# The first unit of a feed-forward layer is split in two halves, with the second unit between them

## The chip, the core and the metric

The kernel is one program on one core of a Trainium2 chip. Its five engines are TensorE (matrix products; PE in the profile, PEld for its loads of weights), VectorE (DVE), ScalarE (ACT), GpSimd (POOL) and SyncE (SP, which only issues DMA transfers here). Engines run side by side, each through its own list of instructions in a fixed order, and wait for each other by semaphores. The metric is the device time of one execution in microseconds.

## The reference, cut to what matters

Three layers in a row, all float32:

```python
# 1. landmark attention: 4 batches, 8 heads, 576 tokens, 64 wide; 32 landmarks
q_lm, k_lm = q.reshape(B,H,32,18,64).mean(3), k.reshape(B,H,32,18,64).mean(3)
A, Bm, C = softmax(q @ k_lm.T / 8), softmax(q_lm @ k_lm.T / 8), softmax(q_lm @ k.T / 8)
Z = Bm.T / (norms of Bm);  6 times: Z = 2*Z - Z @ Bm @ Z
x = (A @ Z @ C @ v)                       # rearranged to 2304 tokens x 512
# 2. feed-forward with mish: 512 -> 2048 -> 512
h = x @ w_in;  x = (h * tanh(softplus(h))) @ w_out
# 3. top-2 of 8 experts, 512 -> 1024 -> 512
noisy = x @ w_gate + softplus(x @ w_noise) * noise
for e in experts: out[tokens of e] += weight * (relu(x @ w1[e]) @ w2[e])
```

## The kernel before, in words

**Products.** Every large product is done in three pieces, with each operand split into a high and a low part (names ending in h and l, and pairs such as `wo`): high x high, high x low, low x high.

**Attention and fold.** For each of the 4 batches, `attention` makes two things. One is a small matrix W (`wt`, written at L571), which takes a serial chain of softmaxes and six products (L548 to L554). The other is the softmax A: `soften` (L415 to L439) ends in the pairs `ah` and `al`. The product A·W·w_in is taken as A·(W·w_in). `fold` makes W·w_in in four blocks `gt` of 512 columns for each batch (L700 on TensorE, L707 on ScalarE, L709 on VectorE).

**Units and steps.** The 2304 tokens are 8 units of 288, and a batch has two units. The feed-forward layer of a unit is 8 steps of 256 of the 2048 hidden columns; step s belongs to unit s // 8. In a step TensorE makes the hidden columns (L733, 12 matmuls; called "up" below), ScalarE and VectorE apply mish (L746 to L771, ending in `gh` and `gl`), and TensorE multiplies by `w_out` (L788 to L790, 24 matmuls; "down"), adding over the 8 steps into four PSUM banks (`ps_acc`). The blocks of w_in and w_out arrive as float64 bits in integers and are rebuilt as float32 on VectorE: L599, L601, L603 (`widen`), and for w_out also L660 and L662. That is done once, during the first units; w_in goes back to device memory and is read again for later batches.

**Routing and experts.** After the last step of a unit, `route` copies the sums out (L839), turns them (L851, 12 transposes), picks two experts for each token (some 40 small VectorE instructions, L877 to L1008) and scatters the rows to per-expert slots in device memory (L1012, GpSimd). `zeros` fills the slots and the output with zeros before, also from GpSimd. From 486 us on, 16 expert jobs of 8 steps follow (L1151 up, L1172 to L1174 down). Each job has a first part of 384 or a second part of 256 slots; `gather` reads its rows, `entries` its list of tokens and weights (`ent`), and `give` scales the result and scatters it into the output (L1181, L1185).

**What sets the order.** Each piece is a coroutine that yields the engine and a rough cost for its next instruction. A planner (`Order.run`) keeps a clock for each engine and takes, of the instructions ready at that time, the one with the earliest due time. Due times come from `due_hidden(s)` and `due_moe(s)` and from the offsets in the table `DU`. The result is a fixed list for each engine. `keep_warm` (L589) puts small matmuls without use wherever TensorE would be free before batch 0 is ready.

Rings bound the buffers: one pair of PSUM banks for up, four banks `acc` for down, three `gh`, four `ld` (loads of q, k, v).

Of the kernel before, what the change touches and what calls it, by code (L numbers as in the profile page):

```python
# [21 lines left out]
U = 288  # L22
# [43 lines left out]
class Order:  # L66
# [105 lines left out]
    w7=0.03, t0=145.6, t1=9, t2=4.8, m0=566.3, win=67.3, wo=4.1, att=84.6, grp=73, sof=-40.6, fet=191.2, fev=157.4,  # L172
    mkU=132.3, fold=-30.7, up=-7.6, down=27.3, mish=22.6, route=-30.6, r6=24.9, r7=-94.1, send=-11.1, rows=-251.1,
    sc=-182.2, sc6=846.5, yT=-119.9, rein=-163.9, rl=-134.9, zero=204.2, w=0, lists=136.5, wts=68.3, spl=-514.8,
    gath=399.6, turn=-379.2, fin=-286.6, part=287.7, mish2=-40.6, mdown=93.9, st1=3, st2=2, st3=2,
# [3 lines left out]
def due_hidden(s):  # L179
    return DU["t0"] + DU["t1"] * min(s, 8) + DU["t2"] * max(s - 8, 0)  # L180
# [34 lines left out]
class Kern:  # L215
# [63 lines left out]
    def fill(self, dst, src, nbytes):  # L279

        yield op("G", 1.1)
        self.nc.gpsimd.dma_start(dst, src)
        yield dma(nbytes)
# [8 lines left out]
    def attention(self, b):  # L292
# [48 lines left out]
        def group(hg):  # L341
# [67 lines left out]
            o.spawn(soften(hg), due - DU["sof"])  # L409
# [33 lines left out]
        def make_AT():  # L443
            tk = yield get(self.r_AT, 2)
            for i in range(2):
                self.t_AT[2 * b + i] = tk + i
                self.AT[2 * b + i] = (
# [56 lines left out]
        o.spawn(make_AT(), due - DU["sof"])  # L504
# [104 lines left out]
    def conv_in(self):  # L609
# [24 lines left out]
        for i in range(4, 16):  # L634
# [5 lines left out]
            o.spawn(widen(i // 4, i % 4, raw, self.r_raw, tk, [1]), due_hidden(i // 2) - DU["win"])  # L640

    def reload_in(self):
        for b in range(1, B):
            for fb in range(4):
                for c in range(4):
                    yield wait(self.kept[fb, c])
                    self.o.cur.late = due_hidden(16 * b + 2 * fb) - DU["rein"]
# [4 lines left out]
    def conv_out(self):  # L652
# [13 lines left out]
        for f in range(NF):  # L666
# [10 lines left out]
            o.spawn(split(f, raw, t, ring, tk), due_hidden(f // 2) + DU["down"] - DU["wo"])  # L677


    def fold(self):  # L680

        o, V, A, T = self.o, self.V, self.A, self.T
        for b in range(B):
            yield wait(self.got_WT[b])
            for fb in range(4):
                o.cur.late = due_hidden(16 * b + 2 * fb) - DU["fold"]
# [28 lines left out]
    def hidden(self, s):  # L715

        o, V, A, T, P = self.o, self.V, self.A, self.T, self.np_
        u, f = s // (NF // 2), 2 * (s % (NF // 2))
# [8 lines left out]
        for i in range(2):  # L727
            yield op("T", 0.772)
# [9 lines left out]
        if u % 2 and f % 4 == 2:  # L738
            o.put(self.r_gt, self.t_gt[b, fb])
# [37 lines left out]
        if f == 0:  # L777
            self.t_acc = yield get(self.r_acc, 4)
            self.acc = [self.bank("acc") for _ in range(4)]
        acc = self.acc  # L780
        for i in range(2):
            yield wait(self.got_wo[f + i])
            hi, lo = self.wo[f + i]
            for c in range(4):
                if c % 2 == 0:
                    yield op("T", 0.737)
                n = slice(128 * c, 128 * c + 128)
                T.matmul(acc[c][:, :U], hi[:, n], gh[:, i], start=f + i == 0, stop=False)  # L788
                T.matmul(acc[c][:, :U], hi[:, n], gl[:, i], start=False, stop=False)  # L789
                T.matmul(acc[c][:, :U], lo[:, n], gh[:, i], start=False, stop=f + i == NF - 1)  # L790
# [14 lines left out]
    def zeros(self):  # L805


        yield wait(self.downed[2])
# [5 lines left out]
        for i, c in enumerate(range(0, CAP, U)):  # L814
            n = min(U, CAP - c)
            for e in range(NE):
                dst = slots[e, c : c + n].rearrange("(n p) x -> p n x", p=min(n, 96))
                src = zero[: min(n, 96)].unsqueeze(1).broadcast_to([min(n, 96), max(n // 96, 1), D + LW])
                yield from self.fill(dst, src, n * 4 * (D + LW))
            self.o.set(self.filled[i])  # L820
        yield wait(self.downed[20])
# [6 lines left out]
    def route(self, u, acc, ta):  # L828
# [8 lines left out]
        for c in range(4):  # L837
            yield op("A", cp(U), DU["yT"] - self.o.cur.late + due_hidden(8 * u + 7))
            A.copy(yT[:, c, :], acc[c][:, :U])  # L839
            o.put(self.r_acc, ta + c)  # L840

        def send():
# [4 lines left out]
            for i in range(3):  # L847
                for q in range(4):
                    yield op("V", cv(384), DU["rows"] if u >= NU - 2 else 0.0)
# [5 lines left out]
        o.spawn(send(), due_hidden(8 * u + 7) + DU["send"])  # L855
        yield wait(self.routed[u - 1] if u else self.emptied)
        if u < len(self.filled):
# [598 lines left out]
```

## Time and profile before

| | us |
|---|---|
| median of 3 runs | 966.08 (962.16 to 966.98) |
| the profiled execution | 968.66 |
| span of its instructions | 966.8 |
| TensorE busy | 914.0 |
| VectorE busy | 625.7 |
| ScalarE busy | 457.6 |

The span runs from the first to the last instruction; the execution is 1.9 us longer than its span, and 2.6 us longer than the median. TensorE's busy time counts the warm-up matmuls before 57 us, and matmuls are pipelined, so a busy stretch is not the same as a full one. The granted clock is given as a share of 2.4 GHz: 0.50 is 1.2 GHz.

### The profile page before, as it was taken

What the parts mean: (1) busy time and instruction counts of PE and PEld (TensorE: products, weight loads), DVE (VectorE), ACT (ScalarE), POOL (GpSimd) and SP (SyncE); (2) the same over time, 40 slices, a digit from 0 to 9 for tenths busy, and PEclk for the clock granted to TensorE, in tenths of its full rate; (3) what the DMA queues carried; (4) which work ended last, traced back from release to release, by engine and by line L of the source; (5) the groups of instructions that cost most, each with busy time, mean ns of one, the idle gap of its engine ahead of it and who ended that gap; (6) DMA issues with size and microseconds to landing.
All of it is one profiled execution on the core that took longest, in us unless ns stands there. A gap on an engine that the chain in (4) does not pass through costs nothing. (4 is left out here: it accounts for less than half of the span.)

```text
span 966.8 us, 18134 instructions
## 1 busy us (share of the span) xinstructions
PE 914.0 (95%) x7135; PEld 799.1 (83%) x7135; DVE 625.7 (65%) x1519; ACT 457.6 (47%) x825; POOL 136.4 (14%) x129
## 2 busy tenths in 40 slices
PE   9979768999999998999999989999999999999995
PEld 7767656878886877889898979899989899999984
DVE  6999689566986669486958466646565555445411
ACT  2247655667766686588853233333333223323210
POOL 0002100223101200202020412101121011111102
PEclk9989989999999999999999999999999999999998
DMA  8677950565406410323243667666556355464103
GB/s 303 198 256 255 360 209 3 152 192 173 194 7 200 164 53 2 115 67 86 58 153 91 153 191 162 148 169 143 135 118 158 109 111 125 98 165 94 17 3 51
DMA packets 70075, 131.62 MB, mean 136 GB/s; under 512 B 13696, under 2 KB 34784, under 8 KB 69984
## 3 DMA queue, kind: packets, MB, share of 16 engines
q1 hardware_dynamic: 56960, 96.16, 32.6%
q0 software_dynamic: 13024, 34.25, 15.1%
q8 instruction: 58, 0.95, 0.4%
q14 instruction: 33, 0.27, 0.1%
HBM read 91.94 MB, written 39.48 MB: 136 GB/s over the span
## 5 line engine op out<-in xcount | busy, mean ns | idle before, releaser
L1151 PE MATMUL ps_up<-xh,mw 128*128 128x256 f32 (+1 forms) x1024 | 265.5, 312 | 2.8 <-ACT mw L1039 2.1
L1151 PEld LDWEIGHTS ps_up<-xh,mw 128*128 128x128 f32 x1024 | 183.1, 189 | 15.5 <-ACT mw L1039 2.5
L1160 ACT ACTIVATE gh<-ps_up 128x384 fp32r<-128x384 f32 (+1 forms) x128 | 56.1, 438 | 285.7 <-PE ps_acc L1173 161.6
L1162 DVE SCALAR_TENSOR_TENSOR gl<-ps_up,gh 128x384 fp32r<-128x384 f32 (+1 forms) x128 | 62.7, 490 | 170.1 <-ACT gh L1160 169.9
L788 PE MATMUL ps_acc<-gh,wo 128*128 128x288 f32 x512 | 159.2, 311 | 5.3 <-ACT gh L768 5.0
L1151 PE MATMUL ps_up<-xl,mw 128*128 128x384 f32 (+1 forms) x512 | 159.3, 311 | 0.0
L789 PE MATMUL ps_acc<-gl,wo 128*128 128x288 f32 x512 | 153.2, 299 | 2.8 <-DVE gl L771 2.8
L790 PE MATMUL ps_acc<-gh,wo 128*128 128x288 f32 x512 | 152.7, 298 | 0.2 <-DVE wo L662 0.2
L733 PE MATMUL ps_h<-ah,gt 128*128 128x288 f32 x512 | 127.3, 306 | 15.7 <-ACT mh L746 15.2
L1172 PE MATMUL ps_acc<-mw,gh 128*128 128x512 f32 x320 | 126.5, 395 | 0.0
L1173 PE MATMUL ps_acc<-mw,gh 128*128 128x512 f32 x320 | 126.4, 395 | 0.0
L1174 PE MATMUL ps_acc<-mw,gl 128*128 128x512 f32 x320 | 125.8, 393 | 0.0
L1185 POOL DMA_INDIRECT out<-yp,off x40 | 67.0, 1674 | 376.9 <-DVE yp L1181 278.3
L788 PEld LDWEIGHTS ps_acc<-gh,wo 128*128 128x128 f32 x512 | 97.9, 191 | 25.5 <-issue 13.2
L733 PEld LDWEIGHTS ps_h<-ah,gt 128*128 128x128 f32 x512 | 90.0, 191 | 32.5 <-ACT mh L746 21.5
L1151 PEld LDWEIGHTS ps_up<-xl,mw 128*128 128x128 f32 x512 | 96.7, 189 | 10.0
L789 PEld LDWEIGHTS ps_acc<-gl,wo 128*128 128x128 f32 x512 | 98.0, 191 | 3.8 <-DVE gl L771 3.8
L1041 DVE TENSOR_TENSOR mw<-mraw,mw 128x1024 fp32r<-128x1024 f32 x72 | 87.8, 1223 | 18.5 <-ACT mw L1039 17.9
L790 PEld LDWEIGHTS ps_acc<-gh,wo 128*128 128x128 f32 x512 | 97.9, 191 | 0.4 <-DVE wo L662 0.4
L1012 POOL DMA_INDIRECT slots<-rr,sl x48 | 47.7, 994 | 336.4 <-DVE rr L1008 319.4
L1039 ACT CAST mw<-mraw 128x1024 fp32r<-128x1024 f32 x72 | 74.6, 1042 | 3.4 <-DMA mraw<-in_ew 3.4
L733 PE MATMUL ps_h<-al,gt 128*128 128x288 f32 x256 | 76.0, 297 | 0.0
(189 smaller groups left out, 1384.9 us busy)
## 6 DMA issues: line engine op xcount, KB each, us to landing
mraw<-in_ew SPq DMA_DIRECT2D x72, 512.0 KB, 4.1
win<-win_d SPq DMA_DIRECT2D x48, 256.0 KB, 3.4
xg<-slots SPq DMA_DIRECT2D x160, 64.0 KB, 3.1
slots<-zero POOLq DMA_DIRECT2D x16, 580.5 KB, 20.0
raw<-in_w_in SPq DMA_DIRECT2D x16, 512.0 KB, 4.7
raw<-in_w_out SPq DMA_DIRECT2D x16, 512.0 KB, 6.3
kT<-in_kT SPq DMA_DIRECT2D x8, 576.0 KB, 6.9
qT<-in_qT SPq DMA_DIRECT2D x8, 576.0 KB, 7.3
```

Source lines behind the costliest of these rows:

```text
L733: T.matmul(hp[:, i, :U], gt[:, x, hg, n : n + 128], AT[y][:, hg, :], start=k == 0, stop=k == 5)
L788: T.matmul(acc[c][:, :U], hi[:, n], gh[:, i], start=f + i == 0, stop=False)
L789: T.matmul(acc[c][:, :U], hi[:, n], gl[:, i], start=False, stop=False)
L790: T.matmul(acc[c][:, :U], lo[:, n], gh[:, i], start=False, stop=f + i == NF - 1)
L1039: self.A.copy(w[:, 0], raw)
L1041: self.V.tensor_tensor(out=w[:, 1], in0=raw, in1=w[:, 0].bitcast(F32), op=OP.subtract)
L1151: T.matmul(h[:, :n], w[:, i, 128 * c : 128 * c + 128], x[j][:, c, :n], start=k == 0, stop=k == 11)
L1162: self.V.scalar_tensor_tensor(out=gl[:, :n], in0=hp[:, :n], scalar=0.0, in1=gh[:, :n].bitcast(F32), op0=OP.max, op1=OP.subtract)
L1172: T.matmul(a, g[0][:, n], w[:, 0, 512:], start=first, stop=False)
L1173: T.matmul(a, g[0][:, n], w[:, 1, 512:], start=False, stop=False)
L1174: T.matmul(a, g[1][:, n], w[:, 0, 512:], start=False, stop=last)
L1185: st = self.G.indirect_dma_start(out=self.out[:, :], out_offset=bass.IndirectOffsetOnAxis(ap=off[:, b : b + 1], axis=0), in_=y, in_offset= ...
```

## The change

The step order is now a list `STEPS`: the first four steps of unit 0, all eight of unit 1, the last four of unit 0, and then units 2 to 7 as before. The four sums of the first half of unit 0 are copied from PSUM to a buffer of the ring `ld` (`set_aside`, four ScalarE copies), and added again when unit 0 ends (four VectorE additions in place of four ScalarE copies). Unit 1 is routed before unit 0. The zero fill covers only the second part of each expert's slots, 8 transfers of 516 KB each, and starts after step 5 in place of step 2. The due times and costs are new numbers, the softmax A of batch 0 has a due time of its own (`sof0`), and so have the expert lists (`ent`).

```diff
 DU = dict(
-    w7=0.03, t0=145.6, t1=9, t2=4.8, m0=566.3, win=67.3, wo=4.1, att=84.6, grp=73, sof=-40.6, fet=191.2, fev=157.4,
+    w7=0.4, t0=-24.6, t1=8.83, t2=2.01, m0=786.2, win=-65.7, wo=-244.7, att=486.3, grp=199.1, sof=-304.1,
...
+STEPS = [(0, f) for f in range(0, NF // 2, 2)] + [(1, f) for f in range(0, NF, 2)] + [(0, f) for f in range(NF // 2, NF, 2)]
+STEPS += [(u, f) for u in range(2, NU) for f in range(0, NF, 2)]
+UNITS = [1, 0] + list(range(2, NU))
...
-            o.spawn(soften(hg), due - DU["sof"])
+            o.spawn(soften(hg), due - DU["sof0" if head else "sof"])
...
-        if f == 0:
+        if begin:
             self.t_acc = yield get(self.r_acc, 4)
...
+        if end and f < NF - 2:
+            ts = yield get(self.r_ld)
+            o.spawn(self.set_aside(acc, self.t_acc, ts), due_hidden(s) + DU["down"] - DU["sp"])
...
+    def set_aside(self, acc, ta, ts):
+        part = self.ap.tile([128, 2, S], F32, name="part", tag="ld", bufs=4)
+        self.part, self.t_part = part.rearrange("p a (b n) -> p (a b) n", n=U), ts
+        for c in range(4):
+            yield op("A", cp(U))
+            self.A.copy(self.part[:, c], acc[c][:, :U])
+            self.o.put(self.r_acc, ta + c)
...
-        yield wait(self.downed[2])
+        yield wait(self.downed[DU["zst"]])
...
-        for i, c in enumerate(range(0, CAP, U)):
...
+        slots = slots[:, CAPA:].rearrange("e (n p) x -> e p n x", p=128)
+        for e in range(NE):
+            src = zero.unsqueeze(1).broadcast_to([128, CAPB // 128, D + LW])
+            yield from self.fill(slots[e], src, CAPB * 4 * (D + LW))
...
-            yield op("A", cp(U), DU["yT"] - self.o.cur.late + due_hidden(8 * u + 7))
-            A.copy(yT[:, c, :], acc[c][:, :U])
+            if u:
+                yield op("A", cp(U), late)
+                A.copy(yT[:, c, :], acc[c][:, :U])
+            else:
+                yield op("V", 0.37, late)
+                V.tensor_tensor(out=yT[:, c, :], in0=acc[c][:, :U], in1=self.part[:, c], op=OP.add)
...
-            self.o.spawn(self.job_entries(j), due_moe(FE * j + 4))
+            self.o.spawn(self.job_entries(j), due_moe(FE * j + 4) - DU["ent"])
```

Three places show what the new order is. In the changed program line numbers are higher by 19 to 39: L619 to L623 are `widen`, L720 and L729 the fold, L755 up, L810 to L812 down.

**TensorE, before the first step.** Before, the third fold block (`ps_g_778`) and the first up step (`ps_h_867`), with 49 pairs of warm-up rows between them, of which one stands:

```order
L700 MATMUL ps_g_778<-win_465,wt_665 32x512 x2
L700 MATMUL ps_g_778<-win_546,wt_665 32x512 x2
L589 LDWEIGHTS onesb_82
L589 MATMUL ps_h_128<-onesb_82 96x256
...
L733 MATMUL ps_h_867<-ah_136,gt_697 128x288
L733 MATMUL ps_h_867<-al_137,gt_697 128x288
```

Now, from the last warm-up on:

```order
L609 LDWEIGHTS onesb_82
L609 MATMUL ps_h_128<-onesb_82 96x256
L720 MATMUL ps_g_683<-win_145,wt_650 32x512 x2
L720 MATMUL ps_g_683<-win_187,wt_650 32x512 x2
L720 MATMUL ps_g_701<-win_310,wt_650 32x512 x2
L720 MATMUL ps_g_701<-win_375,wt_650 32x512 x2
L755 MATMUL ps_h_721<-ah_138,gt_682 128x288
```

No warm-up matmul stands between the folds any more (219 in place of 325 in all), and the first up step follows the second fold block.

**VectorE, batch 0.** Before, the softmax results `al` stand behind both parts of the first fold (`gt_697`):

```order
L709 TENSOR_TENSOR gt_697<-ps_g_728,gt_697 128x512
L603 SCALAR_TENSOR_TENSOR win_710<-raw_657,win_710 128x512
L423 TENSOR_SCALAR sA_127<-sA_127 128x18
L427 TENSOR_TENSOR A1_291<-A1_291,sA_127 128x576
L425 RECIPROCAL sA_127<-sA_127 128x18
L432 STREAM_TRANSPOSE Af_794<-A1_291 128x576
...
L439 TENSOR_TENSOR al_139<-Af_811,ah_138 128x288
```

Now they stand inside the six products of W (`X2`):

```order
L574 SCALAR_TENSOR_TENSOR X2_572<-X2_551,ps_g_557 128x192
L458 TENSOR_TENSOR al_139<-Af_540,ah_138 128x288
L623 SCALAR_TENSOR_TENSOR win_310<-raw_186,win_310 128x512
L574 SCALAR_TENSOR_TENSOR X2_592<-X2_572,ps_g_578 128x192
L458 TENSOR_TENSOR al_137<-Af_504,ah_136 128x288
...
L729 TENSOR_TENSOR gt_682<-ps_g_701,gt_682 128x512
```

The softmax moved ahead of the fold, and nine or ten blocks of weights that stood ahead of it moved behind it.

**VectorE, W of batch 1.** Before, W (`wt_2087`) stands among the routing of unit 0 (`rd`, `sa`, `sl`):

```order
L977 TENSOR_SCALAR rd_2113<-pk_2100 96x6
L980 SCALAR_TENSOR_TENSOR rd_2113<-pk_2100,rd_2113 96x6 x2
L771 SCALAR_TENSOR_TENSOR gl_2117<-mh_1897,gh_2110 128x576
L983 SCALAR_TENSOR_TENSOR sa_2127<-ek_1929,pk_2100 96x6
L571 COPY wt_2087<-ps_g_2114 128x2x32
L986 SCALAR_TENSOR_TENSOR sl_2145<-rd_2113,sa_2127 96x6
L571 COPY wt_2087<-ps_g_2115 128x2x32
```

Now it stands among the last blocks of w_out, and the first transposes of a route (`rr`) come behind it:

```order
L621 SCALAR_TENSOR_TENSOR t_1754<-raw_1753,t_1754 128x512
L591 COPY wt_1841<-ps_g_1842 128x2x32
L775 TENSOR_SCALAR me_1865<-mh_1852 128x576
L591 COPY wt_1841<-ps_g_1843 128x2x32
...
L682 TENSOR_TENSOR wo_117<-raw_1845,wo_117 128x512
...
L890 STREAM_TRANSPOSE rr_2011<-yT_1977 32x4x3x32
```

The first route moved from before W of batch 1 to behind it; part of w_out moved the other way.

## Rows read from the trace of the kernel before

**Rows 1.** Busy time by stage (stretch, length, engines, PE clock, DMA share, GB/s).

```profile
0.00:57.00 57.00, 55.76 (x631) 44.17 (x631) 46.88 (x113) 12.70 (x30) 1.39 (x11) 1.00 0.74 254
57.00:174.00 117.00, 90.34 (x872) 75.27 (x876) 100.59 (x226) 74.91 (x136) 9.78 (x14) 0.93 0.58 204
181.00:300.00 119.00, 116.42 (x1165) 99.15 (x1165) 82.27 (x220) 76.94 (x148) 24.46 (x31) 0.99 0.47 155
507.00:967.00 460.00, 446.23 (x2532) 401.04 (x2530) 238.22 (x531) 139.87 (x233) 73.60 (x46) 0.99 0.50 118
```

**Rows 2.** The same view, the stretches around batch 1.

```profile
67.00:71.00 4.00, 3.72 (x14) 3.40 (x15) 3.98 (x8) 2.46 (x5) 0.00 (x0) 0.50 0.92 314
115.00:132.00 17.00, 5.29 (x28) 4.82 (x26) 9.83 (x16) 6.99 (x11) 0.00 (x0) 0.80 1.00 381
132.00:174.00 42.00, 35.13 (x480) 28.70 (x484) 37.84 (x115) 24.28 (x49) 0.00 (x0) 0.96 0.06 21
```

**Rows 3.** TensorE in time: start, length, engine, line, what, count, wait before.

```profile
51.25 5.64 PE L589 MATMUL ps_h<-onesb 128*96 128x256 bf16 x49
57.05 0.37 PE L733 MATMUL ps_h<-ah,gt 128*128 128x288 f32 x1
67.10 0.61 PE L788 MATMUL ps_acc<-gh,wo 128*128 128x288 f32 x1 [4.65 <-ACT gh L768]
180.70 0.30 PE L790 MATMUL ps_acc<-gh,wo 128*128 128x288 f32 x1
180.84 0.29 PE L733 MATMUL ps_h<-ah,gt 128*128 128x288 f32 x1
508.23 0.94 PE L866 MATMUL ps_g<-wgn,yT 128*32 128x16 f32 x72
```

**Rows 4.** Who TensorE waited for, 120 to 200 us (sum, times, longest).

```profile
PE ps_h L733 <- ACT mh L746: 7.8, 1, 7.8
PE ps_g L356 <- DVE ql L327: 4.5, 1, 4.5
```

**Rows 5.** VectorE in time: fold, softmax result, w_out block, W of batch 1.

```profile
49.23 0.68 DVE L709 TENSOR_TENSOR gt<-ps_g,gt 128x512 fp32r<-128x512 f32 x1
56.26 0.45 DVE L439 TENSOR_TENSOR al<-Af,ah 128x288 fp32r<-128x288 f32 x1
118.77 0.43 DVE L599 TENSOR_SCALAR raw<-raw 128x512 int32<-128x512 int32 x1 [5.63 <-DMA raw<-in_w_out]
173.40 0.21 DVE L571 COPY wt<-ps_g 128x64 f32<-128x64 f32 x1
```

**Rows 6.** Who VectorE waited for, 57 to 175 us.

```profile
DVE raw L599 <- DMA raw<-in_w_out: 5.6, 1, 5.6
DVE ql L327 <- DMA qT<-in_qT: 1.6, 1, 1.6
DVE kl L327 <- DMA kT<-in_kT: 1.2, 1, 1.2
```

**Rows 7.** Groups by line, whole span: busy us, mean ns of one, idle before.

```profile
L851 DVE STREAM_TRANSPOSE rr<-yT 32x384 f32<-32x384 f32 x96 | 54.6, 568 | 12.3 <-DMA slots<-rr,sl 5.9 <-ACT yT L839 4.2
L763 DVE SCALAR_TENSOR_TENSOR mh<-me,mh 128x576 f32<-128x576 f32 x64 | 48.3, 754 | 18.5 <-ACT me L761 17.6
L603 DVE SCALAR_TENSOR_TENSOR win<-raw,win 128x512 int32<-128x512 int32 x16 | 10.9, 682 | 0.0
L901 DVE TENSOR_REDUCE m<-nz 96x3 f32<-96x24 f32 x16 | 2.7, 167 | 0.2
L839 ACT COPY yT<-ps_acc 128x288 f32<-128x288 f32 x32 | 12.2, 400 | 5.4 <-PE ps_acc L790 5.4
```

**Rows 8.** DMA issues: transfer, queue, count, KB of one, us to landing.

```profile
slots<-zero POOLq DMA_DIRECT2D x16, 580.5 KB, 20.0
ent<-slots SPq DMA_DIRECT2D x8, 6.0 KB, 4.1
```

**Rows 9.** Who TensorE waited for, 500 to 600 us.

```profile
PE ps_up L1151 <- ACT mw L1039: 2.1, 1, 2.1
```

More of the change, by code (lines that the diff above doesn't have):

```diff
@@ L171, with first, last_of @@
 DU = dict(
[L172 to L175 removed]
+    w7=0.4, t0=-24.6, t1=8.83, t2=2.01, m0=786.2, win=-65.7, wo=-244.7, att=486.3, grp=199.1, sof=-304.1,
+    fet=257.9, fev=58.6, mkU=153.2, fold=27.3, up=-50.3, down=-14.1, mish=-15.0, route=-92.7, r6=101.7, r7=682.0,
+    send=202.4, rows=-900, sc=94.3, sc6=897.1, yT=-473.0, rein=-280.7, rl=217.1, zero=279.7, w=0.02, lists=392.0,
+    wts=175.3, spl=-347.7, gath=446.0, turn=-496.0, fin=-159.3, part=152.9, mish2=291.8, mdown=337.6, st1=1,
+    st2=1, st3=1, t3=3.09, sp=379.3, sof0=131.7, zst=5, zot=17, ent=-467.4,
 )
 def due_hidden(s):
[L180 removed]
+    return DU["t0"] + DU["t1"] * min(s, 4) + DU["t3"] * min(max(s - 4, 0), 8) + DU["t2"] * max(s - 12, 0)
+STEPS = [(0, f) for f in range(0, NF // 2, 2)] + [(1, f) for f in range(0, NF, 2)] + [(0, f) for f in range(NF // 2, NF, 2)]
+STEPS += [(u, f) for u in range(2, NU) for f in range(0, NF, 2)]
+UNITS = [1, 0] + list(range(2, NU))
+END = {u: STEPS.index((u, NF - 2)) for u in UNITS}
+AT_F = {f: min(s for s, (u, g) in enumerate(STEPS) if g == f // 2 * 2) for f in range(NF)}
+def first(b, fb):
+    return min(s for s, (u, f) in enumerate(STEPS) if u // 2 == b and f // 4 == fb)
+def last_of(b, fb):
+    return max(s for s, (u, f) in enumerate(STEPS) if u // 2 == b and f // 4 == fb)
 def due_moe(s):
@@ L503, in attention @@
         o.spawn(make_U(), due - DU["mkU"])
-        o.spawn(make_AT(), due - DU["sof"])
+        o.spawn(make_AT(), due - DU["sof0" if head else "sof"])
         for hg in range(2):
@@ L646, in reload_in @@
                     yield wait(self.kept[fb, c])
-                    self.o.cur.late = due_hidden(16 * b + 2 * fb) - DU["rein"]
+                    self.o.cur.late = due_hidden(first(b, fb)) - DU["rein"]
                     yield from self.chunk_in(fb, c)
@@ L685, in fold @@
             for fb in range(4):
-                o.cur.late = due_hidden(16 * b + 2 * fb) - DU["fold"]
+                o.cur.late = due_hidden(first(b, fb)) - DU["fold"]
                 self.t_gt[b, fb] = yield get(self.r_gt)
@@ L727, in hidden @@
         for i in range(2):
[L728 removed]
+            yield op("T", 0.786)
             n = 128 * (f % 4 + i)
@@ L813, in zeros @@
         slots = self.slots[: NE * CAP].rearrange("(e c) x -> e c x", e=NE)
-        for i, c in enumerate(range(0, CAP, U)):
[L815 to L821, printed above, removed]
+        slots = slots[:, CAPA:].rearrange("e (n p) x -> e p n x", p=128)
+        for e in range(NE):
+            src = zero.unsqueeze(1).broadcast_to([128, CAPB // 128, D + LW])
+            yield from self.fill(slots[e], src, CAPB * 4 * (D + LW))
+        self.o.set(self.filled)
+        yield wait(self.downed[DU["zot"]])
         rows = self.out.rearrange("(p n) x -> p n x", p=128)
@@ L1286, in run_all @@
         self.routed_a = Event()
-        self.filled = [Event() for _ in range(0, CAP, U)]
+        self.filled = Event()
         self.AT, self.WT, self.win, self.gt = {}, {}, {}, {}
```

40 lines of the change are left out of this document (23 added, 17 removed).

## The prediction

> **What bounds the kernel now.** I read the chip's time by stage first, then what TensorE waited for, then what VectorE did there. In the expert stage (507 to 967 us) TensorE is busy 446.2 of 460 us, and between 181 and 300 us 116.4 of 119 [rows 1]: both are TensorE's, and a faster VectorE buys nothing there. Between 57 and 174 us it is not so. TensorE is busy 90.3 of 117 us, VectorE 100.6 [rows 1], and the two longest stalls lie side by side in 115 to 132 us, where TensorE works 5.3 of 17 us [rows 2]: 7.8 us for ScalarE's mish, which itself waits for VectorE, and 4.5 us for the split queries of batch 1 [rows 4]. VectorE works only 9.8 us of those 17 [rows 2]. It waited 5.6 us for a block of w_out, which ended at 118.8 us [rows 5], and 1.6 and 1.2 us for the queries and keys of batch 1 [rows 6], while the DMA engines were busy the whole time (share 1.00 [rows 2]) with the zero fills: 16 transfers of 580.5 KB, 20.0 us each from issue to landing [rows 8]. So the path up to W of batch 1 is VectorE's list, stretched by a DMA jam. W is written at 173.4 us [rows 5]; only then can W·w_in of batch 1 be folded, and step 16, the first of batch 1, starts at 180.84 us [rows 3]. From there on TensorE is the limit. What the change is worth is therefore: how much earlier W of batch 1 is ready, less the TensorE work that has been pushed behind that point.
>
> **The change part by part.**
>
> *VectorE's work ahead of W of batch 1.* Before, 46.9 us of it lie in 0 to 57 and 100.6 in 57 to 174 [rows 1], in all 147.5 of 174 us; 26.5 us are idle, 10.1 of them before 57. Counted in the two orders, the new list has these fewer instructions ahead of W: the 12 transposes of the first route (12 x 0.568 = 6.8 us [rows 7]); 29 small routing instructions (the nearest row is 0.167 us [rows 7], 4.8 at most); two mish products and one of the pairs' low parts (3 x 0.754 = 2.3 [rows 7]); and six blocks of weight rebuilding (6 x 0.68 = 4.1 [rows 7]). That is 18.0 by durations; neighbouring small instructions overlap by some hundredths of a microsecond, and I take 16. Nothing of it vanishes, it only comes later: between 181 and 300 us VectorE is busy 82.3 of 119 us [rows 1], so 36.7 are free to take 16.
>
> *The fill.* 8 x 516 KB = 4.1 MB in place of 16 x 580.5 KB (9.3 MB) and eight smaller ones: about 0.4 of the bytes. It also starts after step 5 instead of step 2, and in the new order of the queues the loads of batch 1's second keys and queries are issued ahead of it, so that they are not caught in it. VectorE's 8.4 us of DMA waits [rows 6] go to 0.4 of that, 3.4 us, a gain of 5.0. From below, all 8.4 could go; from above, the w_out block may still meet the fill and none go. The other 8.0 us of idle time after 57 us and the 10.1 before it I leave as they are.
>
> So W comes 16 + 5.0 = 21.0 us earlier, at about 153 us.
>
> *TensorE's debt.* At step 16 the old order has done 13 of the 16 down steps and one route's products; the new one 12 and none. One down step is 24 matmuls, of which two neighbours start 0.14 us apart (180.70 and 180.84 [rows 3]), 3.4 us; a route's products are 0.94 us [rows 3]. These 4.3 us of work are still owed: 21.0 - 4.3 = 16.7 us. If TensorE has idle time later to hide them, nothing is lost, but there are only 2.6 us in 181 to 300 [rows 1], so I charge all.
>
> *Setting the sums aside.* Four ScalarE copies of 0.40 us [rows 7] and four VectorE additions in place of four copies. ScalarE is busy 74.9 of 117 us [rows 1] and hides them. What TensorE feels is one more hand-over of the four banks, in which the first copy has to be done before a bank is used again: 0.4 us. If that cover is gone, all four: 1.6. An up step and a fold block stand between the two down steps in the order, so the cost could also be zero. The buffer taken from `ld` until unit 0 ends leaves three for loads of batch 1 and 2; should a load of batch 1 wait for it, it would add to the idle time of VectorE, which the range holds.
>
> *The start.* Before, warm-ups run from 51.25 to the first up step at 57.05 [rows 3], because the softmax result that the step needs ends at 56.7 [rows 5], after the second part of the fold at 49.9 [rows 5]. Now the softmax stands ahead of the fold, and the first step should begin at 48 to 50 us. I cost this at nothing of its own: the stretch is VectorE's, and the work it does first is already in the sum. A gain here would appear only as VectorE idling less.
>
> *The expert stage.* Its first step waits 2.1 us for weights [rows 9]; the last routing is spread differently, and I take half of it, 1.0, as gained; bounds 2.1 lost or gained. Then 446.2 us of TensorE work [rows 1] are the same.
>
> Sum: 16.7 - 0.4 + 1.0 = 17.3 us off the profiled execution's 968.66, which gives 951.4. That execution was 2.6 us above the median of the three runs, 966.08, so the median should be 966.08 - 17.3 = 948.8, say 949.
>
> Bounds. The best for W: of the 16.4 us idle after 57 only 5 stay (11.4 gained) and half the idle time of the head goes with the earlier start (5): 16 + 11.4 + 5 - 4.3 = 28.1, and 2.1 at the experts: 30.2, 936. The worst without a new mechanism: no idle time goes, 16 - 4.3 - 1.6 = 10.1, and 2.1 lost at the experts: 8.0, 958.
>
> **The rivals.**
>
> *More of the idle time goes (932 to 943).* For it: TensorE and ScalarE had work for VectorE 8 us earlier, and the old 8.0 us of other idle time are hand-overs in a chain with only one or two steps in flight. With no route in between, mish now follows mish. Against it: the weights still have to come in at 16 + 16 blocks, with the DMA engines 74% busy before 57 us [rows 1].
>
> *The DMA jam moves and stays (about 962 to 968, no change).* The DMA share is already high before the fill [rows 1], and a fill of 4.1 MB still keeps the engines full for some 10 us at the 381 GB/s of rows 2. If the w_out loads and the earlier loads of batch 2 meet in it, VectorE idles 8.4 us as before and another 8.4 beside, and 10.1 - 8.4 = 1.7 are left: 964. By the Trainium skill ("DMA: Bandwidth & Descriptors", section "Queues, rings and completion order"), a DMA engine takes turns packet by packet between the queues that have work. By that rule a load is slowed as long as any fill is under way, and it is the time of the fill, not its place behind, that counts; a load issued within it is no faster than before. Rows 6 and 8 agree with such sharing: the loads crept rather than stopped. I give it little, since the fill is shorter by 0.6.
>
> *TensorE falls to its lower clock at the early start (955 to 963).* The clock was granted at 0.50 in 67 to 71 us [rows 2], 1.2 GHz, right behind a gap of 4.65 us in TensorE's work [rows 3]. With the warm-ups cut off at 48 us and folds and up steps waiting for VectorE, gaps of that size may recur between 45 and 60 us, and work there takes twice as long. The Trainium skill ("TensorE: Matmul & The Clock Gate", "What's actually happening") says that the throttled state is the default and activity releases it; the drop at 67 us agrees. Against a price: TensorE has some 9 us of work in that stretch, so at half speed it loses at most 9 us, and it waits for VectorE there anyway. 949 + 9 = 958.
>
> *The lists of the experts come too late (slower).* The lists of tokens and weights now have a due time 467 later than their place in the job. VectorE's scaling of a job's result and so TensorE's four banks wait for the list. A list lands in 4.1 us [rows 8]; with the 1 us of instructions around it a late one costs a job about 5.5 us of TensorE. The gain of 17 is used up from the fourth of 16 jobs on; eight late jobs cost 44, and 966 - 17 + 44 = 993. Against it: in the two orders the list instructions stand at the same expert step, within one.
>
> **How the numbers follow.** My forecast, 943 to 955, has 58%; more idle time gone (932 to 943) 18%; the lower clock or small losses (955 to 962) 10%; no change 7%; late lists or another mechanism that makes it slower 7%. The likeliest is 949; its own range 943 to 955. Leaving out the late lists, the jam and the last few of the best case, the range is 934 to 962. A measurement can tell 0.5%, 4.8 us, from no change: faster is below 961.2, slower above 970.9. So faster 0.85, same 0.08, slower 0.07.
>
> **What would show it.** Right: the first up step starts at 48 to 50 us; VectorE writes W of batch 1 near 153 us and step 16 starts about 160 to 164; the waits of 7.8 and 4.5 us are below 3 each; the fill's transfers take well under 20 us each; in 181 to 300 TensorE stays busy above 97%; the expert stage lasts as long as before, within 2 us. Wrong: W of batch 1 is written at 165 us or later (the idle time has moved, or the softmax moved the fold back), or the earlier step 16 is given back before 507 us because VectorE, with the route behind it, is late for the mish of steps 16 to 24; or TensorE waits for `yp` or the lists in the expert stage.

## The result and the profile after

| | before | changed |
|---|---|---|
| median, us | 965.78 (962.16 to 966.98, 4 runs) | 951.27 (950.15 to 955.68, 4 runs) |
| the profiled execution | 968.66 | 950.15 |
| span | 966.8 | 948.3 |

The changed kernel takes 0.9865 of the time, with a 95% interval of 0.9824 to 0.9905: 14.5 us less between the medians, 18.5 between the two profiled executions. Measured a second time, beside the experiments, it was 0.9845 (0.982 to 0.987).

The stages of the changed kernel, with the columns of [rows 1]:

```profile
0.00:57.00 57.00, 52.77 (x560) 37.86 (x560) 46.89 (x112) 15.80 (x36) 1.38 (x11) 0.91 0.66 238
57.00:143.00 86.00, 76.53 (x720) 63.00 (x721) 82.82 (x174) 64.05 (x121) 6.07 (x8) 0.98 0.68 235
57.00:174.00 117.00, 106.67 (x1006) 86.63 (x1007) 108.72 (x234) 87.65 (x162) 6.07 (x8) 0.99 0.59 203
115.00:132.00 17.00, 16.84 (x216) 15.24 (x215) 16.44 (x45) 13.46 (x27) 4.08 (x6) 1.00 0.97 345
181.00:300.00 119.00, 113.00 (x1198) 95.71 (x1199) 90.88 (x236) 78.51 (x147) 22.45 (x24) 0.99 0.43 147
490.00:948.00 458.00, 440.61 (x2444) 396.37 (x2442) 236.94 (x535) 136.34 (x229) 74.05 (x46) 0.99 0.49 118
```

In 57 to 174 us TensorE is busy 106.7 of 117 us (90.3 before [rows 1]) and VectorE 108.7 (100.6). In 115 to 132 us, where TensorE worked 5.3 us [rows 2], it now works 16.8, though the DMA engines are just as full (0.97). The next two views show who TensorE waited for in 57 to 174 us, and who VectorE waited for in 57 to 144 us (sum, times, longest):

```profile
PE ps_h L755 <- ACT mh L768: 3.6, 2, 2.1
PE ps_g L409 <- DVE gt L729: 1.9, 1, 1.9
PE ps_acc L812 <- DVE wo L682: 1.6, 2, 1.4
PE ps_acc L810 <- ACT wo L680: 1.6, 2, 0.9
```

```profile
DVE gl L793 <- ACT gh L790: 2.0, 4, 1.2
DVE t L619 <- DMA raw<-in_w_out: 0.5, 1, 0.5
DVE gt L729 <- ACT gt L727: 0.3, 1, 0.3
DVE wo L682 <- ACT wo L680: 0.3, 1, 0.3
```

The stalls of 7.8 and 4.5 us [rows 4] are gone (the longest wait for mish that is left is 2.1 us), and of VectorE's 8.4 us of DMA waits [rows 6] 0.5 are left. Four marks in time (start, length, engine, line, what):

```profile
42.53 0.40 PE L755 MATMUL ps_h<-ah,gt 128*128 128x288 f32 x1
142.82 0.21 DVE L591 COPY wt<-ps_g 128x64 f32<-128x64 f32 x1
152.87 0.29 PE L755 MATMUL ps_h<-ah,gt 128*128 128x288 f32 x1
194.74 2.31 DVE L890 STREAM_TRANSPOSE rr<-yT 32x384 f32<-32x384 f32 x4 [4.37 <-DMA slots<-rr,sl]
```

The first up step starts at 42.5 us (57.05 [rows 3]), W of batch 1 is ready at 143.0 (173.6 [rows 5]), and step 16 starts at 152.87 (180.84 [rows 3]). A transfer of the fill now takes 9.8 us from issue to landing (median; 20.0 [rows 8]). The last mark is where part of the lead is lost again: VectorE waits 4.4 us with transposes of the second routed unit, for scatters of the first. At the start of the expert stage (470 to 560 us) TensorE waits for VectorE and ScalarE, where before it had 2.1 us [rows 9]:

```profile
PE ps_up L1190 <- DVE mw L1080: 3.2, 4, 1.4
PE ps_up L1190 <- DVE gl L1201: 2.1, 1, 2.1
PE ps_up L1190 <- ACT mw L1078: 1.7, 1, 1.7
```

To see where the time goes I count, for each kernel, TensorE's work done by a time: every matmul that has started, warm-ups left out, at the mean interval between starts on its line in the kernel before. How waits are kept out of that mean moves an entry by 1 to 2 us, and differences along a row by less. The lead over the kernel before's trace, in us:

| by | 60 | 100 | 140 | 180 | 200 | 240 | 300 | 480 | 560 | 600 us |
|---|---|---|---|---|---|---|---|---|---|---|
| changed | 4.0 | 1.5 | 15.6 | 23.4 | 18.2 | 20.8 | 18.5 | 23.3 | 17.2 | 21.7 |
| changed, plain steps (e1) | 5.7 | -3.0 | 3.0 | 9.5 | 6.4 | 10.5 | 3.1 | -0.8 | -2.8 | 2.2 |
| changed, full fill (e2) | 4.0 | 1.5 | 15.1 | 15.6 | 13.3 | 14.7 | 7.6 | 8.3 | -1.9 | 3.1 |
| before, smaller fill (e3) | 0.8 | 2.1 | 5.9 | 11.2 | 7.1 | 11.5 | 5.7 | 5.4 | 1.5 | 5.8 |
| before, late route (e5) | 1.3 | 2.4 | -0.7 | 2.3 | 1.6 | -11.1 | -15.6 | -14.6 | -13.9 | -18.9 |
| split after six steps (e6) | 4.0 | 1.7 | 5.5 | 10.2 | 6.5 | 9.2 | 1.8 | -10.1 | -10.1 | -8.2 |
| new steps, old numbers (e9) | 1.7 | 1.0 | 15.8 | 4.9 | -10.7 | -24.1 | -26.3 | -30.1 | -30.7 | -35.2 |

TensorE's last matmul ends at 935.3 us in the changed kernel and at 956.0 before, a lead of 20.7; from there to the end are 13.0 us (10.8 before), which leaves 18.5.

### The profile page after: what moved, and what is told of

Read it like the earlier page. It is cut to its first block, busy times and chain, and to the rows that moved or that the text cites. A ratio compares the mean times of both kernels' runs of the same rounds, so it can differ in the third digit from the quotient of the medians.

```text
span 948.3 us, 17922 instructions
## 1 busy us (share of the span) xinstructions
PE 903.3 (95%) x7029; PEld 785.4 (83%) x7029; DVE 627.6 (66%) x1523; ACT 457.1 (48%) x825; POOL 128.2 (14%) x113
## 5 line engine op out<-in xcount | busy, mean ns | idle before, releaser
L810 PE MATMUL ps_acc<-gh,wo 128*128 128x288 f32 x512 | 161.7, 316 | 2.5 <-ACT wo L680 1.6
L812 PE MATMUL ps_acc<-gh,wo 128*128 128x288 f32 x512 | 152.0, 297 | 1.6 <-DVE wo L682 1.6
L755 PE MATMUL ps_h<-ah,gt 128*128 128x288 f32 x512 | 126.8, 306 | 12.5 <-ACT mh L768 9.7
L810 PEld LDWEIGHTS ps_acc<-gh,wo 128*128 128x128 f32 x512 | 97.1, 190 | 30.0 <-issue 19.3
L1224 POOL DMA_INDIRECT out<-yp,off x40 | 65.1, 1628 | 350.7 <-DVE yp L1220 269.3
L755 PEld LDWEIGHTS ps_h<-ah,gt 128*128 128x128 f32 x512 | 90.7, 193 | 25.2 <-ACT mh L768 14.6
L1190 PEld LDWEIGHTS ps_up<-xl,mw 128*128 128x128 f32 x512 | 96.3, 188 | 10.5
L812 PEld LDWEIGHTS ps_acc<-gh,wo 128*128 128x128 f32 x512 | 97.1, 190 | 2.0 <-DVE wo L682 2.0
L1051 POOL DMA_INDIRECT slots<-rr,sl x48 | 50.8, 1058 | 347.4 <-DVE rr L1047 224.8
L755 PE MATMUL ps_h<-al,gt 128*128 128x288 f32 x256 | 76.6, 299 | 0.0
```

The costliest lines, as they stand in the source:

```text
L755: T.matmul(hp[:, i, :U], gt[:, x, hg, n : n + 128], AT[y][:, hg, :], start=k == 0, stop=k == 5)
L810: T.matmul(acc[c][:, :U], hi[:, n], gh[:, i], start=begin and i == 0, stop=False)
L1190: T.matmul(h[:, :n], w[:, i, 128 * c : 128 * c + 128], x[j][:, c, :n], start=k == 0, stop=k == 11)
L1224: st = self.G.indirect_dma_start(out=self.out[:, :], out_offset=bass.IndirectOffsetOnAxis(ap=off[:, b : b + 1], axis=0), in_=y, in_offset= ...
```

## The experiments

The experiments ran on different chips. The kernel before took 966.0 us beside e5, e7, e8 and the second run of the changed kernel, 974.3 beside e1 to e4, 977.4 beside e6, e9 and e10, and 977.1 beside e12. So kernels are compared by their ratio to the kernel before on the same chip. The changed kernel was not run on the three slower chips; that its 0.9845 holds there too is taken, not shown.

The eight traces from the slower chips have something that the six taken where before takes 966 us lack: pauses of TensorE, VectorE and ScalarE whose end the profile puts down to no engine and no transfer (`issue` or `remote` where the name of a releaser would stand). Counting those over 0.3 us, a trace from a slower chip has 9 to 21 of them, 13 to 46 us over the three engines, and the six others have one, of 0.3 us. The first comes at 166 us in e3 and e9, between 189 and 197 in e2, e4, e10 and e12, at 228 in e1 and at 298 in e6. The lead is taken against one trace of before from the faster chip. Up to the first pause it is the kernel's own; behind it the chip's losses are in it too.

**The changed kernel again.**

> The changed kernel unchanged, beside the other kernels of this call, so that they can be compared with it on the same chip. If the gain does not depend on the chip, it is 0.983 to 0.990 of the kernel before.

951.54 us, 0.9845 (0.982 to 0.987). W of batch 1 is ready at 142.4 us, and step 16 starts at 152.2, as in the first trace.

**e1: the changed kernel with plain steps.**

```diff
-STEPS = [(0, f) for f in range(0, NF // 2, 2)] + [(1, f) ...] + [(0, f) for f in range(NF // 2, NF, 2)]
...
-UNITS = [1, 0] + list(range(2, NU))
+STEPS = [(u, f) for u in range(NU) for f in range(0, NF, 2)]
+UNITS = list(range(NU))
```

> The changed kernel, with the steps again in the plain order (unit 0 whole, then unit 1; no sums set aside, route of unit 0 first); its due numbers and its smaller fill stay, and its VectorE list again has no route work ahead of W of batch 1. Theory A (the gain is VectorE's list: W of batch 1 comes early because the route and some weight blocks stand behind it and the DMA waits are gone): W of batch 1 still near 143 us, and the time 948 to 956, as the changed kernel's 951. Theory B (the interleaved steps are the gain: with half of unit 0 and then unit 1 the second half of w_in and w_out is due later, so that TensorE has steps to do while VectorE rebuilds weights): W of batch 1 may be early, but TensorE stalls for weights in 57 to 140 us as before, its lead at 180 us is under 12 us instead of 23, and the time is 958 to 966.

971.39 us, 0.9984 (0.9965 to 1.0003): nearly all the gain is gone, although W of batch 1 is ready at 140.1 us, earlier than in the changed kernel. Its 57 to 115 us, and TensorE's longest waits in 57 to 175:

```profile
57.00:115.00 58.00, 46.08 (x350) 32.68 (x349) 55.88 (x115) 31.97 (x62) 0.00 (x0) 0.85 0.74 248
```

```profile
PE ps_acc L811 <- DVE wo L681: 6.5, 3, 3.3
PE ps_g L374 <- DVE ql L345: 3.6, 1, 3.6
```

VectorE is full (55.9 of 58 us), and TensorE waits for the blocks of w_out that VectorE rebuilds. Step 5 starts at 80.1 us, step 6 at 106.9: all blocks are due within unit 0. The lead at 140 us is 3.0 in place of 15.6. Theory A, by which the time follows W, falls; theory B holds. It does not account for all of the loss: at 240 us half of the changed kernel's lead is still there (10.5 of 20.8), as much as in e3 (11.5), which has the old order and the smaller fill and on the same chip comes to 0.993. What e1 loses beyond that it loses after 240 us, and why is open. Its due numbers were chosen for the interleaved steps; plain steps with numbers of their own that bring W as early were not run.

**e2: the changed kernel with the full zero fill.**

```diff
-        slots = slots[:, CAPA:].rearrange("e (n p) x -> e p n x", p=128)
+        slots = slots.rearrange("e (n p) x -> e p n x", p=128)
...
-            src = zero.unsqueeze(1).broadcast_to([128, CAPB // 128, D + LW])
+            src = zero.unsqueeze(1).broadcast_to([128, CAP // 128, D + LW])
```

> The changed kernel, but each of its 8 zero fills covers both parts of an expert's slots (1290 KB instead of 516 KB, 10.3 MB in all), at the same place in the same order. Theory A (a large part of the gain is that VectorE waits for no DMA any more): the DMA engines stay full for some 15 us longer between 112 and 145 us, the loads of w_out or the next batch come late, VectorE idles 4 to 8 us more before W of batch 1, and the time rises by 3 to 8 us, to 954 to 959. Theory B (only the place of the fill matters, since what is loaded next is issued ahead of it): within 2 us of the changed kernel's 951.

965.69 us, 0.9916 (0.9893 to 0.994): by the ratios about 0.7%, 7 us, of the gain is lost. First VectorE's longest wait, then TensorE's, in 57 to 180 us:

```profile
DVE raw L619 <- DMA raw<-in_w_out: 6.0, 2, 3.6
```

```profile
PE ps_acc L810 <- ACT wo L680: 5.5, 2, 4.6
```

W is only 2.1 us later (145.1), but the last blocks of w_out come late, TensorE stands 4.6 us for one, and the lead stops at 15 where it went on to 23. The size of the fill matters (theory A), and it acts through w_out rather than through W.

**e3: the kernel before with the smaller fill.** The first 288 rows of an expert are not filled, of the next 288 only those of the second part are; the planner is told the old sizes.

```diff
-                yield from self.fill(dst, src, n * 4 * (D + LW))
+                if i == 1:
+                    m = c + n - CAPA
+                    dst = slots[e, CAPA : c + n].rearrange("(n p) x -> p n x", p=96)
+                    src = zero[:96].unsqueeze(1).broadcast_to([96, m // 96, D + LW])
+                yield op("G", 1.1)
+                if i:
+                    self.nc.gpsimd.dma_start(dst, src)
+                yield dma(n * 4 * (D + LW))
```

> The kernel before, with its zero fill cut to the second part of each expert's slots (4.1 MB instead of 10.3 MB, 8 issues fewer), at the old place and with the old order otherwise. Theory A: the 8.4 us in which VectorE waits for w_out and for the queries and keys of batch 1 fall to some 3 us, the stalls of 7.8 and 4.5 us of TensorE shrink with them, and the time falls by 4 to 8 us, to 958 to 962. Theory B (VectorE's work ahead of W decides, the waits are hidden by the chain of mish): under 2 us, 964 to 967.

966.47 us, 0.9928 (0.9902 to 0.9955): by the ratio 7.0 us less than before on that chip, 7.8 between the medians. TensorE's waits in 100 to 200 us that answer to [rows 4]:

```profile
PE ps_h L733 <- ACT mh L746: 3.4, 2, 2.2
...
PE ps_g L356 <- DVE ql L327: 1.9, 1, 1.9
```

The 7.8 and 4.5 us have become 2.2 and 1.9, and W is ready at 162.3 us, 11.3 earlier. Theory A holds: by the ratios (0.9928 and 0.9845) the fill alone is about half of the change's gain.

**e4: the zero fills of the output later.**

```diff
-            yield from self.fill(rows[:, n : n + 3], ..., 786432)
+            yield op("G", 0.7)
+            yield dma(786432)
+        yield wait(self.downed[24])
+        for n in range(0, NTOK // 128, 3):
+            self.nc.gpsimd.dma_start(rows[:, n : n + 3], ...)
```

> The changed kernel with the six zero fills of the output (768 KB each) issued after step 24 instead of after step 17; the planner's list stays the same otherwise. Theory A (the stall of 3.9 us at 196 us, where TensorE waits for mish and VectorE waits 4.4 us for a scatter of routed rows, comes from these fills, which keep the DMA engines at a share of 1.0 in 183 to 206 us): both waits fall under 1 us and the time by 3 to 5 us, to 946 to 949. Theory B (the same fills meet a later scatter, or the time is given back in the expert stage): within 1.5 us of 951.

970.17 us, 0.9952 (0.9936 to 0.9968): slower than the changed kernel, which neither theory had. The fills now stand on GpSimd between the third and the fourth scatter of the second routed unit. VectorE's and TensorE's longest waits in 238 to 290 us:

```profile
DVE rr L894 <- DMA slots<-rr,sl: 12.3, 1, 12.3
...
PE ps_g L568 <- DVE z L920: 4.9, 1, 4.9
```

The other scatters queue behind 4.7 MB of fill, and the next unit's transposes wait 12.3 us for the one buffer `rr`. The lead falls from 21.2 at 240 us to 9.3 at 260.

**e5: the kernel before with the first route behind W.**

```diff
         def send():
+            if u == 0:
+                yield wait(self.got_WT[1])
...
+        if u == 0:
+            yield wait(self.got_WT[1])
         tg = yield get(self.r_g)
```

> The kernel before, in which the transposes and the gate products of the first route wait for W of batch 1 (12 transposes, 29 small routing instructions and two mish instructions fewer ahead of W on VectorE, no other change of the order meant). Theory A (my sum: VectorE's work ahead of W is worth its own length): W of batch 1 some 13 us earlier, at about 160 us, and the time 6 to 10 us lower, 0.990 to 0.994 of before. Theory B (the step order makes the gain; what VectorE does while the serial chain of W waits for TensorE and ScalarE costs nothing): W at most 5 us earlier and the time within 0.3% of before.

983.45 us, 1.0173 (1.0142 to 1.0203): slower by 1.7%, outside both theories. The time to W in this kernel, and then VectorE's and TensorE's waits in 205 to 235 us:

```profile
0.00:167.00 167.00, 142.67 (x1398) 116.81 (x1399) 135.59 (x292) 85.41 (x161) 12.97 (x28) 0.93 0.68 237
```

```profile
DVE rr L853 <- DMA slots<-rr,sl: 12.4, 1, 12.4
```

```profile
PE ps_g L700 <- DVE z L881: 5.0, 1, 5.0
PE ps_h L733 <- ACT gt L707: 4.6, 1, 4.6
```

VectorE has 12 us less to do up to W (135.6 against 147.2), but W comes only 6.3 us earlier (167.3): the idle time has grown to 31 us. I read this as about half of the route having lain in time in which VectorE would have waited for the chain of W. Afterwards the two routes stand too close: the second one's transposes wait 12.4 us for the scatters of the first, and TensorE loses 10 us behind them.

**e9: the new steps with the old numbers.** The table `DU` and `due_hidden` are those of before; the step order, the set-aside sums, the smaller fill and the planner's new costs stay.

```diff
-    w7=0.4, t0=-24.6, t1=8.83, t2=2.01, m0=786.2, ...
+    w7=0.03, t0=145.6, t1=9, t2=4.8, m0=566.3, ...
+    sp=379.3, sof0=-40.6, zst=2, zot=20, ent=0,
```

> The changed kernel (step order, sums set aside, smaller fill) with the due numbers of before, no due times of its own for the softmax and the expert lists, and the fills after steps 2 and 20 again. Its VectorE list has both first routes (24 transposes) ahead of W of batch 1. Theory A (the interleaved steps are the gain by themselves, since with them half of the weights is due later and TensorE has steps to do): the lead of TensorE's work at 140 us is over 10 us, and the time is near the changed kernel's, 0.984 to 0.990 of before, although W of batch 1 is written late. Theory B (steps, numbers and lists only work together): W comes at 175 us or later, TensorE runs out of steps of batch 0 before it, and the time is 0.993 to 1.01 of before, no better than the smaller fill alone (0.993).

1007.14 us, 1.0314 (1.0285 to 1.0342). The lead at 140 us is 15.8, the same as in the changed kernel. But W is ready at 207.4 us, and between 140 and 215 us TensorE runs out of steps:

```profile
140.00:215.00 75.00, 45.28 (x548) 32.39 (x546) 44.65 (x158) 14.39 (x39) 15.78 (x18) 0.66 0.25 81
```

It is busy 45 of 75 us, much of it at 1.2 GHz (mean 0.66). Part of this is the chip's: TensorE has five pauses of the kind named above, 7.9 us in all, between 161 and 174 us and one of 4.5 us right before W. Without them W would still not come before some 195 us (my estimate, 207.4 less these 12.4). Theory A is right on the lead and wrong on the time; theory B holds. How much of the loss beyond what it said is the kernel's is not shown.

**e6: the split after six steps.** `range(0, NF // 2, 2)` becomes `range(0, 12, 2)`, and the rest of unit 0 begins at 12.

> The changed kernel with unit 1 put behind six steps of unit 0 instead of four (the last two steps of unit 0 follow unit 1). If the gain is that the second half of the weights is due later (theory A), six steps leave it between the plain order (0.998) and the changed kernel (0.985), at 0.988 to 0.994, with TensorE's waits for weights in 80 to 120 us coming back in part. If the gain is in the order of the lists and not in the place of the split (theory B), it is within 0.2% of the changed kernel.

978.66 us, 1.0014 (0.9994 to 1.0033): no gain is left, as with plain steps. W is ready at 141.7 us; TensorE's longest wait in 57 to 175 us is for mish, and there is one for w_out again:

```profile
PE ps_h L755 <- ACT mh L768: 7.1, 7, 3.0
PE ps_acc L812 <- DVE wo L682: 2.6, 2, 2.4
```

The lead at 140 us is 5.5. This goes further than theory A. At 240 us a lead of 9.2 is left; the rest goes behind that, where this chip's pauses lie as well (from 298 us on). The numbers were chosen for a split after four, so a split after six with its own numbers may do better; that was not run.

**e8: warm-up matmuls in the waits of the first step.**

```diff
+                    for _ in range({2: 4, 3: 14, 5: 8}.get(k, 0) if s == 0 and i == 0 else 0):
+                        T.matmul(hp[:96, 1, :256], self.onesb[:, :96], ..., start=True, stop=True)
                     T.matmul(hp[:, i, :U], gt[:, x, hg, n : n + 128], ...)
```

> The changed kernel with 26 warm-up matmuls of 0.11 us put into the waits of the first up step (43 to 47 us), so that TensorE has no gap there. Theory A (my clock rival: the 10 us at a granted clock of 0.50, 46 to 56 us, cost time): the clock stays at 1.00 in 46 to 56 us, W of batch 1 comes 2 to 4 us earlier and the time falls by 2 to 4 us. Theory B (VectorE sets the pace there, 12.3 of 14.5 us busy in 42.5 to 57): the clock is 1.00, W moves under 1 us and the time under 1.5 us.

951.37 us, 0.9848 (0.9825 to 0.9871), as the changed kernel (0.9845). First two stretches of the changed kernel, then one of this:

```profile
44.00:46.00 2.00, 0.53 (x2) 0.30 (x2) 1.92 (x4) 1.04 (x2) 0.00 (x0) 1.00 1.05 394
46.00:48.00 2.00, 1.73 (x9) 0.48 (x9) 1.51 (x3) 0.00 (x0) 0.00 (x0) 0.52 0.78 309
```

```profile
46.00:56.00 10.00, 7.35 (x52) 4.75 (x50) 8.88 (x18) 5.19 (x10) 0.00 (x0) 1.00 0.81 281
```

The clock stays at 1.00 where it had been 0.50 for 10 us, and W is ready at 143.7 us in place of 142.4. Theory B: the lower clock came and cost nothing, since VectorE (8.9 of 10 us busy) sets the pace.

**e7: the zero fills of the output ahead of all scatters.**

```diff
+    def zero_out(self):
+        yield wait(self.downed[11])
+        zero = self.wp.tile([128, D + LW], F32, name="zero2", tag="raw", bufs=2)
+        self.V.memset(zero, 0.0)
...
+            self.nc.gpsimd.dma_start(rows[:, n : n + 3], ...)
```

> The changed kernel with the six zero fills of the output (768 KB each) held back by a second zero tile, written after step 11, so that they run at about 155 to 175 us, ahead of all scatters, instead of between the scatters of the first two routed units; the rest of the lists is the same but for one more memset of VectorE. Theory A (the stall of 4 us at 196 us is a collision of three kinds of transfers: scatters, output fills and the keys and queries of batch 2): VectorE's wait of 4.4 us for a scatter and TensorE's stall fall under 1.5 us, and the time is 2 to 5 us below the changed kernel's. Theory B (the fills then delay the reload of w_in for the folds of batch 1, or the earlier time is given back at the start of the expert stage): within 1.5 us of the changed kernel or slower.

952.47 us, 0.9865 (0.984 to 0.9889). The fills are gone from 183 to 206 us, and the waits are not (VectorE, then TensorE):

```profile
183.00:206.00 23.00, 19.12 (x195) 17.60 (x195) 13.48 (x23) 11.93 (x19) 4.55 (x5) 0.93 0.52 187
```

```profile
DVE rr L898 <- DMA slots<-rr,sl: 4.3, 1, 4.3
...
PE ps_h L755 <- ACT mh L768: 3.9, 1, 3.9
```

With a DMA share of 0.52 in place of 1.01 VectorE waits 4.3 us (4.4) and TensorE 3.9 (3.9). The output fills were not the cause (the loads of batch 2 stayed, so their part was not tried): the buffer of six scatters in a row comes free that late without them too, and a transpose that needs it stands ahead of mish.

**e10 and e12: the transposes behind mish.** In e10 the transposes of the second routed unit wait for step 22, and the planner orders all that follows anew; in e12 five transposes move behind two mish instructions in VectorE's list, and no other instruction moves.

```diff
         def send():
+            if u == 0:
+                yield wait(self.upped[22])
```

```diff
-                    V.transpose(dst, src[32 * q : 32 * q + 32, i])
+                    held.append((dst, src[32 * q : 32 * q + 32, i]))
+                    if u == 0 and 4 * i + q < 5:
+                        continue
+                    for d, x in held:
+                        V.transpose(d, x)
+                    held.clear()
```

> The changed kernel, in which the transposes of the second routed unit wait for the up matmuls of step 22, so that two mish instructions stand ahead of them on VectorE at 190 us. Theory A (the stall of 3.9 us of TensorE at 196 us is VectorE's list: a transpose that waits for the scatters of the unit before stands ahead of mish, whose inputs are there): the stall falls under 1 us, and the time by 2 to 4 us, to 0.981 to 0.984 of before. Theory B (TensorE's lead is given back further on, where it waits for weights at the start of the expert stage): the stall is gone, but the time stays within 0.2% of the changed kernel's.

> The changed kernel with one move in VectorE's list and no other: the first five transposes of the second routed unit stand behind the two mish instructions that followed them (at 190 to 198 us), so that nothing that waits for scatters stands ahead of mish there. Theory A (TensorE's lead of 23 us at 180 us is given back by 4 to 5 us at this one place): the stall of 3.9 us of TensorE falls to 2 us or less, the lead at 200 to 480 us is 2 to 3 us larger than the changed kernel's, and the time is 0.981 to 0.984 of before. Theory B (ScalarE, which is late with mish behind the same place, or the expert stage with its own waits takes it back): the lead at 220 us, or at the latest at 520 us, is the changed kernel's, and the time is 0.9845 to 0.987 of before.

e10: 963.45 us, 0.9855 (0.9821 to 0.9888). e12: 965.56 us, 0.9868 (0.9836 to 0.99). Neither is shown to beat the changed kernel. TensorE's wait in e12, 185 to 210 us, was 3.9 us at one place:

```profile
PE ps_h L755 <- ACT mh L768: 3.4, 2, 2.3
```

The stall has become 2.3 us, ending at 192 us, and 1.1, ending at 207. The first of the two is not the move's. ScalarE stands before the `gh` ahead of it for 3.6 us, released by nothing that the profile names; e10 has the same pause (3.5 us), and so have e2 and e4 (2.8 and 2.7), whose lists are the changed kernel's there. In the changed kernel ScalarE waited 1.15 us at this place, for TensorE. First the changed kernel, then e12:

```profile
187.73 0.69 ACT L790 ACTIVATE gh<-mh 128x576 fp32r<-128x576 f32 x1 [1.15 <-PE ps_acc L812]
189.84 0.68 ACT L790 ACTIVATE gh<-mh 128x576 fp32r<-128x576 f32 x1 [3.58 <-remote]
```

The lead of e12 at 220 us is 19.5 (20.7 in the changed kernel), with these 2.3 us in it. What the move is worth is open: the times fit theory B, but a pause that the faster chip's traces do not have cost TensorE 2.2 to 2.3 us at this very place in both runs, and neither was run on the faster chip. No run beat the changed kernel.

## Why the prediction was right, and where it was not

The median came to 951.27 us where 949 was the likeliest, inside 943 to 955, and the profiled execution to 950.15 against 951.4. The signs came out less well. The two waits (2.1 us at most) and the fill's transfers (9.8 us) were as said. The first up step (42.5 us, not 48 to 50), W (143.0, not 153) and step 16 (152.9, not 160 to 164) were earlier. TensorE was busy 95.0% of 181 to 300 us, not above 97, and the stretch behind 480 us took 4.8 us longer, not the same within 2. So the time is right in part by luck, as the terms show.

*What bounds the kernel* was read rightly as far as the jam of 115 to 132 us and VectorE's list go, and e3 shows that the jam alone was worth 7 us. That the time follows W was not: in e1 W came 33.5 us earlier than before, and the time fell by 0.2%.

*VectorE's work ahead of W*: 16 us were predicted. Measured, VectorE is busy 129.7 us up to 143.0 (46.9 + 82.8 of the rows above) against 147.2 up to 173.6, which is 17.5. The count was right. The step behind it, that such work is worth its own length, was not: in e5 nearly the same work moved (12 us) and W came 6.3 us earlier.

*The fill and the idle time*: this is the term that was mis-sized. I let 16.4 us of idle time between 57 us and W fall by 5.0; it fell by 13.2, to 3.2 (86 - 82.8). The DMA waits went from 8.4 to 0.5, not to 3.4, and of the other 8.0 us 2.7 are left. I had listed this as the first rival (18%) and kept it out of the sum. So W was ready 30.6 us earlier instead of 21.0. The idle time of the head stayed at 10.1, as predicted.

*TensorE's debt*: 4.3 us predicted. The lead at 180 us is 23.4, 7.2 less than 30.6. The 4.3 are in this (12 down steps and no gate products before step 16, 13 and one route's before); beside them step 16 follows W by 9.8 us in place of 7.2, with TensorE busy on steps of batch 0 in between.

That nothing is lost further on was wrong. At 183 to 206 us the lead falls from 23.4 to 18.2; before has its own stall a little later, so that at 240 us 20.8 are left, 2.6 lost. The expert stage, for which I added 1.0, loses 2.6 between 480 us and the last matmul (waits of 3.2, 2.1 and 1.7 us), and the end behind the last matmul is 2.2 us longer. 16.7 - 0.4 + 1.0 = 17.3 was predicted; 23.4 less these three, with 2.5 won back between 240 and 480 us, are the 18.5 of the profiled executions. The two errors, 7 us too little gained up to 180 us and 6 too little lost after it, nearly cancelled, and that is luck. Of the 4.0 us between 18.5 and the medians' 14.5, 2.9 are the profiled execution of before, above its median, and 1.1 that of the changed kernel, below its own.

*Setting the sums aside* cost nothing that TensorE shows: no wait for the banks is in its list of 57 to 174 us.

*The rule that I drew from the profile* ("how much earlier W of batch 1 is ready, less the work pushed behind it") held for this change but is no law. Four kernels set it apart:

| | W of batch 1 early | W late |
|---|---|---|
| plain steps | e1: W 140.1, lead at 140 us 3.0, ratio 0.998 | before: W 173.6, ratio 1 |
| interleaved steps | changed: W 143.0, lead 15.6, ratio 0.985 | e9: W 207.4, lead 15.8, ratio 1.031 |

Of the four, before alone has the full fill; with the smaller one (e3) it is W 162.3, lead at 140 us 5.9, ratio 0.993. An early W in the plain order is paid for by weights that come late. Interleaved steps with a late W give TensorE its lead and then leave it without work. Of these only both together gain more than the smaller fill does by itself, and about half of what they gain needs that fill (e2, e3). The four ran on three chips, and e1 and e9 each have due numbers that were chosen for the other step order, so the table shows that neither half is enough with those numbers, not that no numbers would do. e9 changes all of them at once; which of them the interleaved steps need was not tried.

*The clock* fell, as the rival said and as the Trainium skill has it ("TensorE: Matmul & The Clock Gate", "What's actually happening"): 0.50 in 46 to 56 us, behind waits of the first step. Its price is not to be seen in the time (e8). *The DMA jam*: by the rule of the Trainium skill on queues that take turns ("DMA: Bandwidth & Descriptors", "Queues, rings and completion order") a load within the fill is as slow as before. In the changed kernel the DMA share is 0.97 in 115 to 132 us, yet VectorE waits 0.5 us. The queries and keys were issued ahead of the fill, at 94 us. Two blocks of w_out were issued within it, at 114.7 and 118.7 us, and used at 123.5 and 127.6; the second is the one that came 0.5 us late, nearly 9 us after its issue (median over all 5.8). So a load within the fill was slow, as the rule has it, but here VectorE needed it hardly sooner. In e2, with a longer fill, a load does meet it (3.6 us). *Late lists*: no wait for them is in the expert stage (a late one was priced at 5.5 us; the 4.1 and 1 that it is made of are 5.1).

## What to carry to other kernels

A milestone on the critical path is worth its advance only if the next engine has work to do up to it and after it: count the work done by the engine that sets the end, not the date of the milestone. Before work is moved away from a serial chain, see in the trace whether it lay in the chain's own waits, where it cost nothing, and what it will stand beside at its new place. Zero fills that the result does not need are traffic like any other; leaving them out was the one edit tried that paid by itself.

## What the runs showed of the hardware

The same kernel takes 966.0 us on one chip and 974.3, 977.1 and 977.4 on three others, 0.9 to 1.2% more. No other kernel ran on both, so whether ratios between kernels agree across chips is not shown. The trace of before was not taken on the slower chips, but all eight traces of other kernels there have pauses that the profile puts down to no engine and no transfer (9 to 21 over 0.3 us, the longest 7.1 us), where the six from the faster chip have one in all. What makes them is open. A transpose that needs the buffer of six scatters waited 4.3 to 4.4 us whether the DMA engines were 101% or 52% busy.
